# Quarter loads paced by PE steps in a sparse-attention and soft-MoE kernel on one Trainium2 core

## The chip, the cores and the metric

One core of a Trainium2 chip runs the kernel. The metric is device time in microseconds (us). Engine names follow the profile: PE is TensorE (PEld its weight load), DVE is VectorE, ACT is ScalarE, POOL is GpSimd, SP is SyncE, which issues every DMA here. "us from the start" counts from the first instruction of the profiled span.

## The reference, cut to what matters

The input is a block-sparse attention followed by a soft mixture of experts. All arrays are float32.

```python
# q, k, v: (4 batches, 8 heads, 768, 64); 24 blocks of 32 rows
mask = |block_i - block_j| <= 1, or block 0 or 23 on either side, or one of 3 sampled blocks
attn = softmax(where(mask, q @ k.T / 8, -1e9))
x = (attn @ v) as (3072 tokens, 512)
# soft MoE: 8 experts, 4 slots each; w1 (8, 512, 1024), w2 (8, 1024, 512)
logits = x @ phi                                  # (3072, 32)
slot_in = softmax(logits, over tokens).T @ x      # (32, 512)
slot_out[e] = relu(slot_in[e] @ w1[e]) @ w2[e]
out = softmax(logits, over slots) @ slot_out      # (3072, 512)
```

The weights w1 and w2 hold 33.5 MB; keys and values hold far less.

## The kernel before, in words

The program has two parts. In the first, 52 attention items (13 for each batch b: two "dense" halves, d0 and d1, for the first and the last block of queries, and 11 pairs of sparse query blocks) are computed while the tokens' logits and the slot sums run along. In the second, the expert weights go through PE and the result is combined and stored.

For a sparse pair, POOL and ACT copy the needed blocks of keys from `ktile` into a staging buffer `kst` (lines 365 to 380), PE multiplies (`s`, line 451), DVE takes the row maximum `nm` (466), ACT the exponential `p` (471), DVE turns it over into `ptt` (478), POOL copies sampled blocks of values into `vrs` (396), and PE forms `av` (529). DVE divides it into `x` (525), and PE turns `x` over (`mxt`, 692) for the logits (`ml`, 710) and the slot sums (`ms`, 760). For a dense item the names are `sd` (618), `pd` (637), `ptd` (641) and `avd` (529).

Everything that SP loads passes through its one queue in program order. SP's loads are tracked with eight semaphores in turn (DMAHW0 to DMAHW7 in the listings below), so a load waits until the eighth load before it has landed. These are the loads beside the attention:

- `q` (`load_q`, line 264): 128 KB for each of the 48 items, into four buffers. Each load waits for the PE step that last used the buffer.
- keys (`load_k`, line 274): four loads of 128 rows, 384 KB each, for a batch; two `ktile` buffers.
- values (`load_v`, lines 284 and 287): batches 0 and 1 in eight loads of 128 rows (455 KB, the last ones 260 KB); batches 2 and 3 in 16 loads of 32 rows (113.8 and 65 KB) from `vtab`. The buffers are `v_68` (batches 0 and 2) and `v_69` (1 and 3).
- weights (`load_w`, `load_wk`, line 179): pieces of 512 KB, 128 rows of 4 KB, 64 pieces in all. 22 of them are placed beside the attention: seven in `wpre`, and then, as buffers fall free in the last batch, three in a `ktile` buffer (`kw`), six in `v_68`, three in `ptd` and three in the other `ktile` buffer.

The order of the first part is made by a planner (`Plan.run`). Each task has an engine, an assumed cost, its dependencies, a key and buffers; the planner goes through assumed time and always takes the task that can start first. SP's tasks cost 0.45 to 0.47 us each there. The order that results is what each engine's queue holds, and it is fixed when the program is built.

Code behind the planner loads the other 42 pieces of weights. 15 of them have free room as the attention ends: nine in a pool `lwb`, which lies where the staging buffers of the attention were, and six in `v_69`. The other 27 wait for a buffer that the experts' matmuls (`pf`, line 1055, and `pso`, line 1063) have used up. SP's queue in this part is not written by hand: a scheduler sets the order.

Of the kernel before, what the change touches and what calls it, by code (L numbers as in the profile page):

```python
# [21 lines left out]
P = 128  # L22
NP = 4
# [12 lines left out]
NKST, NVR, NQ = 4, 6, 4  # L36
PB, PTB, XB, XTB = 4, 4, 6, 4
SB, MB = 4, 2

LD0, LD1 = 3, 12  # L40

CS = 2
CW = DM // CS
# [16 lines left out]
class Task:  # L60
    def __init__(self, f, opts, deps, key, acq, byte, pre):
        self.f, self.opts, self.deps, self.key = f, opts, [d for d in deps if d], key
        self.acq, self.byte, self.pre = list(acq), byte, pre
        self.start = self.fin = self.eng = None


class Plan:

    def __init__(self, pools, free):
        self.pools, self.free, self.tasks = pools, free, []

    def add(self, f, opts, deps, key, acq=(), byte=0, pre=None):
        t = Task(f, opts if isinstance(opts, list) else [opts], deps, key, acq, byte, pre)
        self.tasks.append(t)
        return t

    def run(self):
        tasks = self.tasks  # L80
        at = {e: 0.0 for e in LAG}
        dma = 0.0
        left = {t: len(t.deps) for t in tasks}
# [13 lines left out]
        while avail:  # L97
            best = None
            for t in avail:
                r, ok, k = ready[t], True, {}  # L100
                for p, _ in t.acq:
                    i = (nxt[p] + k.get(p, 0)) % self.pools[p]
                    k[p] = k.get(p, 0) + 1
                    if (p in queue and queue[p][0] is not t) or held[p][i]:
                        ok = False
                        break
                    r = max(r, slot[p][i])
                if ok:
                    for e, d in t.opts:
                        c = (max(r, at[e]), t.key, max(r, at[e]) + d)  # L110
                        if best is None or c < best[0]:
                            best = (c, t, e, d)
            assert best, [(t.key, t.opts) for t in avail][:8]
            (st, _, en), t, e, d = best
            avail.remove(t)
            t.start, t.eng, at[e] = st, e, en
            if e == "NONE":
                t.fin = st
            elif e == "SP":
                dma = max(dma, st + 1.4) + t.byte / 0.4e6  # L120
                t.fin = dma + 0.3
            else:
                t.fin = en
# [19 lines left out]

        todo = {e: [t for t in order if t.eng == e and t.pre] for e in at}
        for t in order:
            q = todo[t.eng]
            while q and q[0].start <= t.start + 1.6:
                u = q.pop(0)
                u.vals = u.pre(u.eng)
            t.f(t)  # L150


@with_exitstack
def attn_moe_kernel(ctx, tc, qT, kT, vfull, vtab, sampled, phi, w1, w2, out):
# [19 lines left out]

    def load_w(m, pool, t=None):
        if t is None:
            t = pool.tile([P, WP], F32, name=f"w{m}", tag="w")
        n, j = m // PW, m % PW
        SP.dma_start(out=t, in_=wsrc[n].rearrange("p c f -> p (c f)")[:, j * WP:(j + 1) * WP])
        wtile[m] = t.rearrange("p (c f) -> p c f", f=512 if n < 2 * NE else CW)  # L180

    wk = {}
# [8 lines left out]

    def load_wk(m, tag, j):

        load_w(m + j, None, wk[tag][:, j, :])

# [76 lines left out]

    def load_k(b, p):
        SP.dma_start(out=ktile[b][:, p, :], in_=kT[b, p])

# [3 lines left out]

    def load_v(b, cut, a):  # L280
        lo, hi = cut
        vb = vbuf[b % 2].rearrange("p (a f) -> p a f", a=2)
        if b < 2:
            SP.dma_start(out=vb[:, a, lo:hi], in_=vfull[b, :, a * VH + lo:a * VH + hi])
        else:
            s_ = slice(32 * a, 32 * a + 32)
            SP.dma_start(out=vb[s_, a % 2, lo:hi], in_=vtab[b - 2, s_, lo:hi])
        vtile[b] = vb.rearrange("p a (k r d) -> p a k r d", k=NBZ, r=2)

    def block_numbers(t, i, eng, most):  # L290
# [16 lines left out]
    plan = Plan(dict(s=SB, av=1, pt=MB, p=PB, ptt=PTB, kst=NKST, vrs=NVR, x=XB, xT=XTB, k=2, v=2, q=NQ,  # L307
                     ptd=1, lp=1, dT=1, d=1), free=("pt",))
# [26 lines left out]
    def plan_loads(b):  # L335

        a_k = add(lambda t: new_k(b), ("NONE", 0.0), [qks[first[b - 1] + LD0]] if b else [], -20, acq=[("k", k_use[b])])
        a_v = add(lambda t: None, ("NONE", 0.0), a_k.deps, -20, acq=[("v", v_use[b])])
        pieces = [("k", p) for p in range(NP)] + [("v", *c) for c in v_pieces(b)]
        ks, vs = [], []  # L340
        for m, c in enumerate(pieces):
# [4 lines left out]
            if c[0] == "k":  # L346
                ks.append(add(lambda t, c=c: load_k(b, *c[1:]), ("SP", 0.47), go + [a_k], key, byte=393216))
            else:
                vs.append(add(lambda t, c=c: load_v(b, *c[1:]), ("SP", 0.47), go + [a_v], key,
                              byte=455000 if b < 2 else 114000))  # L350
        t_k[b] = add(lambda t: None, ("NONE", 0.0), ks, -30)
# [899 lines left out]
```

## Time and profile before

| | |
|---|---|
| time, median of 3 runs | 346.43 us (344.92 to 349.33) |
| the profiled execution's own time | 341.82 us |
| its span, first to last instruction | 339.9 us |
| PE busy | 282.2 us, 83% |
| DVE, POOL, ACT busy | 216.7, 180.9, 164.2 us |
| mean granted PE clock | 0.942 |
| moved by DMA | 63.59 MB |
| attention part, to the last `av` | to 259.4 us from the start |
| experts, to the last weight piece's landing | to 320.4 us |

The page gives a share of the span for each engine; a stage has to be looked at by itself, since PE is almost full through the attention, and the DMA engines through the experts. In the chain of waits a piece named "issue" is time in which the engine had work in its program and no semaphore to wait for.

### The profile page before, as it was taken

The page shows a single profiled execution, that of the slowest core. Times are in us where ns is not written, and L with a number is a line of the kernel's source. Part 1 is how long each engine was busy: PE and PEld are TensorE (multiplying, and loading weights), DVE is VectorE, ACT ScalarE, POOL GpSimd, SP SyncE. Part 2 cuts the span into 40 slices and gives each one's busy share as a digit, 9 for nine tenths or more (in the row PEclk, how much of TensorE's full clock was granted, in tenths as well). Part 3 has the DMA queues.
Part 4 walks back from the last instruction along what each step waited for, and adds up shares of the span by engine and source line. Part 5 has one row for each costly group of instructions (what it writes and reads, how often), then busy time and mean ns, then how long its engine had stood idle before and what let it go on. Part 6 is the DMA issues. An engine that isn't in the chain of part 4 may idle for free.

```text
span 339.9 us, 17255 instructions
## 1 busy us (share of the span) xinstructions
PE 282.2 (83%) x7113; PEld 186.9 (55%) x7113; DVE 216.7 (64%) x495; ACT 164.2 (48%) x503; POOL 180.9 (53%) x505
## 2 busy tenths in 40 slices
PE   2697899995989989989999997699785859996650
PEld 0166676762767567776676665476563423453230
DVE  4696778769766998998887896639913430111250
ACT  2656567735646875466767373457500311013240
POOL 2686686984437997946999582648522132000000
PEclk9999999998979999999999999979987659999995
DMA  6942845300753240274341055970529948999987
GB/s 230 397 145 92 286 128 193 102 7 17 230 155 105 78 127 7 53 261 137 98 131 36 2 154 187 320 265 4 189 61 331 384 164 303 415 407 407 381 264 230
DMA packets 29152, 63.59 MB, mean 187 GB/s; under 512 B 3345, under 2 KB 15762, under 8 KB 29074
## 3 DMA queue, kind: packets, MB, share of 16 engines
q1 hardware_dynamic: 29074, 62.49, 54.3%
q8 instruction: 56, 0.92, 1.1%
q14 instruction: 22, 0.18, 0.2%
HBM read 56.19 MB, written 6.29 MB: 184 GB/s over the span
## 4 chain that ended last, share of the span: by engine, by line
PE 60%; DVE 15%; DMA 13%; issue 6%; ACT 2%; SPq 0%; ACTq 0%; POOL 0%; DVEq 0%
PE av L529 28%; PE s L451 11%; PE avd L529 7%; DMA w<-in_w_dram 5%; PE mxt L692 4%; DMA kw<-in_w_dram 3%; PE sd L618 3%; DMA v<-in_w_dram 3%; DVE ptt L478 2%; PE ml L710 2%; DVE ptd L641 2%; DVE nm L466 2%; DVE x L525 2%; DVE nm L630 2%; PE ms L760 1%
## 5 line engine op out<-in xcount | busy, mean ns | idle before, releaser
L396 POOL COPY vrs<-v 128x260 f32 x264 | 95.3, 408 | 31.2 <-PE av L529 24.7
L471 ACT ACTIVATE p<-s,nm 128x256 f32<-128x256 f32 x176 | 71.1, 478 | 16.7 <-DVE nm L466 15.8
L529 PE MATMUL av<-v,ptt 64*64 64x130 f32 (+2 forms) x1728 | 78.2, 294 | 0.4 <-issue 0.4
L478 DVE STREAM_TRANSPOSE ptt<-p 128x512 f32<-128x512 f32 x88 | 58.3, 692 | 17.7 <-ACT p L471 17.6
L529 PEld LDWEIGHTS av<-v,ptt 64*64 64x64 f32 (+2 forms) x1728 | 52.4, 136 | 27.5 <-issue 18.1
L451 PE MATMUL s<-kst,q 64*32 64x256 f32 x1408 | 55.1, 390 | 12.6 <-issue 7.1
L466 DVE TENSOR_REDUCE nm<-s 128x2 f32<-128x512 f32 x88 | 55.5, 677 | 4.7 <-PE s L451 4.3
L372 POOL COPY kst<-ktile 128x384 f32<-128x384 f32 x88 | 42.9, 510 | 20.2 <-PE s L451 17.5
L529 PE MATMUL av<-vrs,ptt 64*32 64x130 f32 x2112 | 45.2, 276 | 5.1 <-issue 5.1
L378 ACT ACTIVATE kst<-ktile 128x128 f32 x171 | 38.9, 302 | 20.3 <-PE s L451 11.0
L451 PEld LDWEIGHTS s<-kst,q 64*32 64x32 f32 x1408 | 30.4, 108 | 28.4 <-issue 13.1
L529 PEld LDWEIGHTS av<-vrs,ptt 64*32 64x32 f32 x2112 | 35.6, 106 | 6.0 <-issue 5.9
L303 ACT COPY xT<-mxt 128x512 f32<-128x512 f32 x20 | 11.7, 586 | 37.9 <-PE mxt L692 37.9
L529 PE MATMUL avd<-v,ptd 64*64 64x130 f32 x768 | 23.6, 271 | 5.0 <-issue 4.4
L637 ACT ACTIVATE pd<-sd,nb 128x384 f32<-128x384 f32 x32 | 16.8, 578 | 19.7 <-DVE nb L632 19.3
L529 PEld LDWEIGHTS avd<-v,ptd 64*64 64x64 f32 x768 | 21.8, 132 | 7.3 <-issue 2.7
L380 POOL COPY kst<-ktile 128x128 f32 x93 | 23.6, 297 | 1.5 <-ACT kst L378 0.7
L618 PE MATMUL sd<-ktile,q 64*32 64x384 f32 x256 | 18.0, 523 | 7.4 <-DMA ktile<-in_kT_dram 6.0
L692 PE MATMUL mxt<-ident,x 128*128 128x128 f32 x96 | 16.8, 301 | 4.0 <-DVE x L525 2.7
L523 DVE TENSOR_SCALAR rs<-av 128x8 f32<-128x8 f32 (+1 forms) x28 | 4.5, 160 | 23.5 <-PE av L529 23.4
L630 DVE TENSOR_REDUCE nm<-sd 128x1 f32<-128x384 f32 x32 | 16.2, 544 | 4.8 <-PE sd L618 4.7
L415 POOL TENSOR_SCALAR q<-q 128x256 f32<-128x256 f32 x21 | 8.5, 407 | 19.4 <-DMA q<-in_qT_dram 19.4
(117 smaller groups left out, 271.2 us busy)
## 6 DMA issues: line engine op xcount, KB each, us to landing
w<-in_w_dram SPq DMA_DIRECT2D x28, 512.0 KB, 7.9
v<-in_w_dram SPq DMA_DIRECT2D x18, 512.0 KB, 6.5
q<-in_qT_dram SPq DMA_DIRECT2D x48, 128.0 KB, 2.7
ktile<-in_kT_dram SPq DMA_DIRECT2D x16, 384.0 KB, 4.7
kw<-in_w_dram SPq DMA_DIRECT2D x12, 512.0 KB, 8.0
v<-in_vfull_dram SPq DMA_DIRECT2D x12, 455.0 KB, 6.1
out_dram<-ob SPq DMA_DIRECT2D x20, 256.0 KB, 4.2
ptd<-in_w_dram SPq DMA_DIRECT2D x6, 512.0 KB, 9.5
```

Source lines behind the costliest of these rows:

```text
L372: POOL.tensor_copy(out=st[:, :, w:w + 96], in_=kv[:, :, (i - 1) * BLK:(i + 2) * BLK])
L378: ACT.activation(out=st[:, :, o:o + BLK], in_=src, func=AF.Copy, scale=1.0)
L380: POOL.tensor_copy(out=st[:, :, o:o + BLK], in_=src)
L396: POOL.tensor_copy(out=st[:, :, j:j + 1, :], in_=vf[:, :, ds(t.vals[j], 1), :])
L451: PE.matmul(u.s[r][32 * p:32 * p + 32, j, :], lhsT=u.q[s_, p, j, :], rhs=kd[j][0][s_, p, :], start=True, stop=True)
L466: DVE.tensor_reduce(out=u.nm[r], in_=u.s[r], axis=AX.X, op=ALU.max, negate=True)
L471: ACT.activation(out=u.p[r][:, j, :], in_=u.s[r][:, j, :], func=AF.Exp, bias=u.nm[r][:, j:j + 1], scale=1.0)
L478: DVE.transpose(out=T.pt[r][:, :, 2 * w:2 * w + 2, :].rearrange("p k j q -> p j k q"), in_=u.p[r].rearrange("p j (k q) -> p j k q", k=8))
L529: PE.matmul(av[o:o + m, g, r * 2 * D1:(r + 1) * 2 * D1].rearrange("p (a d) -> p a d", a=2), lhsT=lhsT, rhs=rhs, start=start, stop=stop)
L618: PE.matmul(u.s[r][k][32 * p:32 * p + 32, :], lhsT=T.dq.q[s_, p, j, :], rhs=kt[s_, p, 384 * k:384 * (k + 1)], start=True, stop=True)
L630: DVE.tensor_reduce(out=nm[:, k:k + 1], in_=u.s[r][k], axis=AX.X, op=ALU.max, negate=True)
L692: PE.transpose(T.px[:, c, :], T.x[:, c * P:(c + 1) * P], ident)
```

## The change

Three things change, and the planner's order with them.

1. The keys of batches 1 to 3, the values of batch 1 and the 22 weight pieces beside the attention are cut into four loads of 32 rows each (`LR = 32`): 96 KB for keys, about 114 or 65 KB for values, 128 KB for weights. Batch 0 stays as it was, and the values of batches 2 and 3 had 32 rows already. SP issues 336 loads where it issued 210.
2. In the planner, a task marked `pace` may not start before the last paced one's start plus its bytes at 0.22 MB per us (`RATE`).
3. A paced load gets a dependency on the last PE step that ends, in the planner's time, by the load's start. The later one of the two `ktile` groups of weights is cut up, though not paced.

```diff
+LR, RATE = 32, 0.22
...
                 if ok:
+                    if t.pace:
+                        r = max(r, paced)
...
             t.start, t.eng, at[e] = st, e, en
+            if t.pace:
+                paced = st + t.byte / RATE / 1e6
...
+        pe = []
         for t in order:
...
-            t.f(t)
+            i = t.f(t)
+            if t.eng == "PE":
+                last = next(i for i in reversed(self.tc.nc.cur_bb.bb.instructions) if i.engine == E_.PE)
+                pe.append((t.fin, last.name))
+            elif t.pace:
+                name = [n for f, n in pe if f <= t.start][-1]
+                self.tc.add_manual_dep(i.ins, name, mybir.DependencyInfo(
+                    mybir.DependencyClass.Sync, mybir.DependencyReason.DATA), reason="pace")
...
-    def load_k(b, p):
-        SP.dma_start(out=ktile[b][:, p, :], in_=kT[b, p])
+    def load_k(b, p, rows):
+        return SP.dma_start(out=ktile[b][rows, p, :], in_=kT[b, p, rows])
...
+        rs = [slice(r, r + LR) for r in range(0, P, LR)] if b else [slice(0, P)]
+        pieces = [("k", p, r) for p in range(NP) for r in rs]
+        pieces += [("v", *c, r) for c in v_pieces(b) for r in (rs if b < 2 else [None])]
...
     for m in range(NPRE):
-        add(lambda t, m=m: load_w(m, wpre), ("SP", 0.45), [qks[max(4, (N - 4) * (m + 1) // (NPRE + 1))]], N + m, byte=524288)
+        for r in range(0, P, LR):
+            add(lambda t, m=m, r=r: load_w(m, wpre, None, slice(r, r + LR)), ("SP", 0.45),
+                [qks[max(4, (N - 4) * (m + 1) // (NPRE + 1))]], N + m + r / P, byte=4096 * LR, pace=True)
...
         for j in range(KW[tag]):
-            add(lambda t, m=m, tag=tag, j=j: load_wk(m, tag, j), ("SP", 0.47), go(j) + [a_w], N + m + j, byte=524288)
+            for r in range(0, P, LR):
+                add(lambda t, m=m, tag=tag, j=j, r=r: load_wk(m, tag, j, slice(r, r + LR)), ("SP", 0.47), go(j) + [a_w],
+                    N + m + j + r / P, byte=4096 * LR, pace=tag != "ktile" or n0 < 12)
```

Three places show what this does to the queues. In the listings a row is one instruction, with its line (line numbers differ by 18 to 27 between the two files), what it writes and reads, and the semaphores that it waits for.

The first is SP's queue where the keys of batch 2 are loaded. Before:

```order
L264 DMA q<-in_qT_dram 128x256 [waits DMAHW6_49,PE_49,Activation_49]
L274 DMA ktile<-in_kT_dram 128x768 [waits DMAHW7_49]
L274 DMA ktile<-in_kT_dram 128x768 [waits DMAHW0_49]
L264 DMA q<-in_qT_dram 128x256 [waits DMAHW1_49,PE_49,Pool_49]
L274 DMA ktile<-in_kT_dram 128x768 [waits DMAHW2_49]
L274 DMA ktile<-in_kT_dram 128x768 [waits DMAHW3_49]
L287 DMA v_68<-in_vtab_dram 32x910 [waits DMAHW4_49,Pool_49]
```

And now:

```order
L283 DMA q<-in_qT_dram 128x256 [waits DMAHW0_49,PE_49,Pool_49]
L293 DMA ktile<-in_kT_dram 32x768 [waits DMAHW1_49,Activation_49]
L293 DMA ktile<-in_kT_dram 32x768 [waits DMAHW2_49,PE_49]
L283 DMA q<-in_qT_dram 128x256 [waits DMAHW3_49,Pool_49]
L293 DMA ktile<-in_kT_dram 32x768 [waits DMAHW4_49]
L293 DMA ktile<-in_kT_dram 32x768 [waits DMAHW5_49]
L293 DMA ktile<-in_kT_dram 32x768 [waits DMAHW6_49]
L293 DMA ktile<-in_kT_dram 32x768 [waits DMAHW7_49]
L293 DMA ktile<-in_kT_dram 32x768 [waits DMAHW0_49]
L293 DMA ktile<-in_kT_dram 32x768 [waits DMAHW1_49]
L283 DMA q<-in_qT_dram 128x256 [waits DMAHW2_49,PE_49,Activation_49]
```

The four loads became 16, of which eight stand ahead of the last `q` shown and the others behind it. A second paced load carries the wait for PE that the `q` load behind it had; most of the others need no PE wait of their own, since an earlier wait in the same queue covers it.

The second is the end of SP's loads beside the attention. Before (`kw` and `v_69` hold weights here, `w_6992` is the first piece of `lwb`):

```order
L179 DMA kw<-in_w_dram 128x1024 [waits DMAHW7_49]
L179 DMA v_69<-in_w_dram 128x1024 [waits DMAHW0_49,Pool_49]
L179 DMA v_69<-in_w_dram 128x1024 [waits DMAHW1_49]
L179 DMA v_69<-in_w_dram 128x1024 [waits DMAHW2_49,PE_49]
L179 DMA v_69<-in_w_dram 128x1024 [waits DMAHW3_49,PE_49]
L179 DMA v_69<-in_w_dram 128x1024 [waits DMAHW4_49,PE_49]
L179 DMA w_6992<-in_w_dram 128x1024 [waits DMAHW5_49,PE_49]
```

And now (`w_7118` is the first piece of `lwb`, `w_7134` the ninth):

```order
L197 DMA kw<-in_w_dram 32x1024 [waits DMAHW5_49]
L197 DMA w_7118<-in_w_dram 128x1024 [waits DMAHW6_49,PE_49,Pool_49]
L197 DMA w_7120<-in_w_dram 128x1024 [waits DMAHW7_49]
L197 DMA w_7122<-in_w_dram 128x1024 [waits DMAHW0_49]
...
L197 DMA w_7134<-in_w_dram 128x1024 [waits DMAHW6_49]
L197 DMA v_69<-in_w_dram 128x1024 [waits DMAHW7_49]
L197 DMA v_69<-in_w_dram 128x1024 [waits DMAHW0_49]
```

Five of the six `v_69` pieces stood ahead of the nine `lwb` pieces; now all six stand behind them. The PE step that the first `lwb` piece waits for is, in both programs, among the last five matmuls of the last `av`.

The third is PE's queue where it first reads the keys of batch 1. Before:

```order
L618 MATMUL sd<-ktile,q 32x384 [waits DMAHW5_49]
L618 MATMUL sd<-ktile,q 32x384
L618 MATMUL sd<-ktile,q 32x384 [waits DMAHW6_49]
L618 MATMUL sd<-ktile,q 32x384
L618 MATMUL sd<-ktile,q 32x384 [waits DMAHW0_49]
```

And now:

```order
L641 MATMUL sd<-ktile,q 32x384 [waits DMAHW6_49,DMAHW5_49]
L641 MATMUL sd<-ktile,q 32x384 [waits DMAHW1_49,DMAHW0_49]
L641 MATMUL sd<-ktile,q 32x384 [waits DMAHW3_49,DMAHW2_49]
L641 MATMUL sd<-ktile,q 32x384 [waits DMAHW5_49,DMAHW4_49]
L641 MATMUL sd<-ktile,q 32x384 [waits DMAHW7_49,DMAHW6_49]
```

Each matmul of a new key tile waits for two quarters where one of two waited for one load. In the whole program PE gets 64 more such wait instructions, 29 of them in the attention and 34 ahead of the experts' first matmuls. Otherwise PE's order of work differs at a few places by one step (an `mxt`, `md` or `sd` moved past its neighbour), and those of DVE, ACT and POOL likewise.

More of the change, by code (lines that the diff above doesn't have):

```diff
@@ L60, with __init__ @@
 class Task:
-    def __init__(self, f, opts, deps, key, acq, byte, pre):
+    def __init__(self, f, opts, deps, key, acq, byte, pre, pace):
+        self.pace = pace
         self.f, self.opts, self.deps, self.key = f, opts, [d for d in deps if d], key
@@ L67, with __init__, add @@
 class Plan:
[L71 to L75, printed above, removed]
+    def __init__(self, tc, pools, free):
+        self.tc, self.pools, self.free, self.tasks = tc, pools, free, []
+    def add(self, f, opts, deps, key, acq=(), byte=0, pre=None, pace=False):
+        t = Task(f, opts if isinstance(opts, list) else [opts], deps, key, acq, byte, pre, pace)
         self.tasks.append(t)
@@ L81, in run @@
         at = {e: 0.0 for e in LAG}
-        dma = 0.0
+        dma = paced = 0.0
         left = {t: len(t.deps) for t in tasks}
@@ L173, in attn_moe_kernel, with load_w @@
     wtile = [None] * NW
-    def load_w(m, pool, t=None):
-        if t is None:
+    def load_w(m, pool, t=None, rows=slice(0, P)):
+        if wtile[m] is None and t is None:
             t = pool.tile([P, WP], F32, name=f"w{m}", tag="w")
+        elif t is None:
+            t = wtile[m].rearrange("p c f -> p (c f)")
         n, j = m // PW, m % PW
-        SP.dma_start(out=t, in_=wsrc[n].rearrange("p c f -> p (c f)")[:, j * WP:(j + 1) * WP])
+        i = SP.dma_start(out=t[rows], in_=wsrc[n].rearrange("p c f -> p (c f)")[rows, j * WP:(j + 1) * WP])
         wtile[m] = t.rearrange("p (c f) -> p c f", f=512 if n < 2 * NE else CW)
+        return i
     wk = {}
@@ L190, in new_wk, with load_wk @@
             wk[tag] = buf[:, 0:k * WP].rearrange("p (k f) -> p k f", k=k)
-    def load_wk(m, tag, j):
-        load_w(m + j, None, wk[tag][:, j, :])
+    def load_wk(m, tag, j, rows=slice(0, P)):
+        return load_w(m + j, None, wk[tag][:, j, :], rows)
     def w_of(n, c):
@@ L278, in v_pieces, with load_v @@
         return [(c, a) for c in cuts for a in range(2 if b < 2 else NP)]
-    def load_v(b, cut, a):
+    def load_v(b, cut, a, rows):
         lo, hi = cut
@@ L283, in load_v @@
         if b < 2:
-            SP.dma_start(out=vb[:, a, lo:hi], in_=vfull[b, :, a * VH + lo:a * VH + hi])
+            i = SP.dma_start(out=vb[rows, a, lo:hi], in_=vfull[b, rows, a * VH + lo:a * VH + hi])
         else:
             s_ = slice(32 * a, 32 * a + 32)
-            SP.dma_start(out=vb[s_, a % 2, lo:hi], in_=vtab[b - 2, s_, lo:hi])
+            i = SP.dma_start(out=vb[s_, a % 2, lo:hi], in_=vtab[b - 2, s_, lo:hi])
         vtile[b] = vb.rearrange("p a (k r d) -> p a k r d", k=NBZ, r=2)
+        return i
     def block_numbers(t, i, eng, most):
@@ L305, in evac @@
             DVE.tensor_copy(out=out, in_=in_)
-    plan = Plan(dict(s=SB, av=1, pt=MB, p=PB, ptt=PTB, kst=NKST, vrs=NVR, x=XB, xT=XTB, k=2, v=2, q=NQ,
+    plan = Plan(tc, dict(s=SB, av=1, pt=MB, p=PB, ptt=PTB, kst=NKST, vrs=NVR, x=XB, xT=XTB, k=2, v=2, q=NQ,
                      ptd=1, lp=1, dT=1, d=1), free=("pt",))
@@ L346, in plan_loads @@
             if c[0] == "k":
-                ks.append(add(lambda t, c=c: load_k(b, *c[1:]), ("SP", 0.47), go + [a_k], key, byte=393216))
+                ks.append(add(lambda t, c=c: load_k(b, *c[1:]), ("SP", 0.47), go + [a_k], key, byte=393216 // len(rs),
+                              pace=b > 0))
             else:
                 vs.append(add(lambda t, c=c: load_v(b, *c[1:]), ("SP", 0.47), go + [a_v], key,
-                              byte=455000 if b < 2 else 114000))
+                              byte=455000 // len(rs) if b < 2 else 114000, pace=b > 0))
         t_k[b] = add(lambda t: None, ("NONE", 0.0), ks, -30)
```

1 line of the change is left out of this document (removed).

## The prediction

> **What bounds the kernel now.** I began with the page. PE is nearly full through the attention, and the last quarter belongs to DMA. The question is what stops PE. The chain of waits tells it: apart from DVE stretches it runs through PE, with pieces called "issue", in which PE had nothing to wait for (start us, us, what; beside them some `av` pieces for comparison).
>
> ```profile
> 26.52 2.10 issue
> ...
> 40.22 1.18 issue
> ...
> 43.04 4.73 PE av L529 x174
> ...
> 54.42 0.37 issue
> ...
> 93.05 1.74 issue
> ...
> 96.31 5.96 PE av L529 x174
> ...
> 105.18 2.35 PE av L529 x88
> ...
> 126.23 0.33 issue
> ...
> 150.48 0.99 issue
> ...
> 203.21 2.33 issue
> ...
> 217.72 3.15 issue
> ...
> 222.94 3.43 PE av L529 x88
> ...
> 243.28 2.33 issue
> ...
> 245.61 4.38 PE av L529 x92
> ...
> 256.49 2.42 issue
> ```
>
> The ten pieces sum to 16.94 us, all on the chain that sets the end. What was SP doing then? Its timeline has large loads just ahead of them:
>
> ```profile
> 199.16 0.42 SPq L179 DMA_DIRECT2D w<-in_w_dram  x1
> ...
> 200.58 1.33 SPq L179 DMA_DIRECT2D kw<-in_w_dram  x2
> ...
> 222.02 0.33 SPq L264 DMA_DIRECT2D q<-in_qT_dram  x1
> ...
> 237.89 1.28 SPq L179 DMA_DIRECT2D kw<-in_w_dram  x3
> 251.68 4.55 SPq L179 DMA_DIRECT2D v<-in_w_dram  x5
> ```
>
> PE has to fetch its program too. By the page's queues and its busy row, that is queue q8:
>
> ```profile
> PE 282.2 (83%) x7113; PEld 186.9 (55%) x7113; DVE 216.7 (64%) x495; ACT 164.2 (48%) x503; POOL 180.9 (53%) x505
> ...
> q8 instruction: 56, 0.92, 1.1%
> ```
>
> 14226 PE and PEld instructions by 56 fetches are 254 to a fetch, 16 KB each. The DMA view of 198.8 to 203.2 us, ahead of a stop, has data and no row for q8:
>
> ```profile
> q1 hardware_dynamic: 338, 0.87, 68.7%
> issues: line engine op xcount, KB each, median us to landing
> ```
>
> The same view of 203.2 to 205.6, the stop itself, has the fetch, and PE goes on as that stretch ends:
>
> ```profile
> q1 hardware_dynamic: 299, 0.74, 89.2%
> q8 instruction: 1, 0.02, 2.4%
> ```
>
> Now the opposite case, 161 to 175 us, with eight loads of 32 rows, four of `q` and one weight piece:
>
> ```profile
> q8 instruction: 4, 0.07, 2.0%
> ...
> q<-in_qT_dram SPq DMA_DIRECT2D x4, 128.0 KB, 2.4
> w<-in_w_dram SPq DMA_DIRECT2D x1, 512.0 KB, 3.9
> v<-in_vtab_dram SPq DMA_DIRECT2D x4, 113.8 KB, 2.7
> ```
>
> Four fetches came and the chain has no stop there. So I read the stops as code fetches that came late behind several large loads in flight at once.
>
> [...]
>
> **The change, part by part.** The profiled execution took 341.82 us, 1.9 more than its span; the sum is made against that. The median of the runs is 346.43, 4.61 higher, and I add this at the end.
>
> *The stops.* In SP's new order at most ten paced loads stand between two `q` loads, and SP needs some 0.42 us to issue one, as for the `w` load above. What does a piece of 512 KB take when the engines are full? Two views of the experts' part, SP's timeline and the chain:
>
> ```profile
> 259.35 6.42 SPq L179 DMA_DIRECT2D w<-in_w_dram  x9
> ...
> 278.99 4.18 SPq L179 DMA_DIRECT2D w<-in_w_dram  x5
> ...
> 297.17 2.83 SPq L179 DMA_DIRECT2D kw<-in_w_dram  x3
> ```
>
> ```profile
> 281.27 6.88 DMA w<-in_w_dram
> ...
> 310.20 10.18 DMA w<-in_w_dram
> ```
>
> SP goes at the pace of landings there: the issues step by 1.25 to 1.28 us ((2.83 - 0.33) / 2 for `kw`). From the third of the 27 pieces, landed at 288.15, to the last at 320.38 the mean is 1.34. A quarter of a piece is 0.32 to 0.34 us of work, issued every 0.42, so no queue builds up; three whole pieces issued in 1.28 us are 3.8 to 4.0 us of work and do build one. The last stop, at 256.49, stood behind `v` pieces that are now queued behind the last `av`. The pace itself changes less: most quarters go out where the whole load went. Bounds: all 16.94 us gone, or none. I take a rest of 0.35 us for each of the ten, as at 54.42 and 126.23: gain 13.4.
>
> *The slow clock.* Three stops are followed by a stretch at half the clock, such as this one from 221.9 to 225.3 (after the busy times: PEclk, DMA share, GB/s); the rows below it serve the next item.
>
> ```profile
> 221.90:225.30 3.40, 3.40 (x38) 2.50 (x44) 1.91 (x3) 2.32 (x9) 3.00 (x9) 0.50 1.00 320
> ```
>
> ```profile
> 72.00:86.00 14.00, 10.47 (x275) 6.05 (x261) 12.37 (x31) 5.87 (x13) 8.69 (x24) 0.88 0.05 14
> 110.00:123.00 13.00, 12.32 (x386) 8.01 (x366) 11.95 (x26) 10.76 (x39) 11.17 (x32) 1.00 0.38 109
> 123.00:163.00 40.00, 38.51 (x1176) 27.52 (x1174) 35.66 (x84) 24.40 (x74) 29.62 (x85) 1.00 0.36 108
> ```
>
> `av` x174 took 5.96 there against 4.73, x88 3.43 against 2.35, and x92 4.38 against 2.46 (2.35 by 92/88): 4.2 us. The stops at 26.52 and 203.21 had no such sequel, so it isn't sure that a stop alone decides. Bounds 0 and 4.2; I take two thirds, 2.8.
>
> *Given back to DVE.* In the three stretches just shown DVE is busy 12.37 of 14, 11.95 of 13 and 35.66 of 40 us. What PE gains before 163 us is 6.71 of stops less 2.1 of rest, and 0.8 of clock: 5.4. PE may then wait for DVE instead. Bounds 0 and 5.4; a third: loss 1.8.
>
> *New waits on PE.* 64 more, of 51 ns by the row for `av`:
>
> ```profile
> L529 PEldq EVENT_SEMAPHORE  x27: 51/51/1096, 17.5 to 240.6; - x27
> ```
>
> The 34 ahead of the experts hide under the weights' arrival (uncovered: 1.7 us). The 29 in the attention have no cover, since PE is full: loss 1.5.
>
> *`q` behind paced loads.* Twelve or so `q` loads now stand one issue behind a quarter that waits for the same PE step: 0.42 us each, 5 in all. POOL and ACT wait for `q`, then `kst` or `p`, then PE. They are busy 53% and 48%, and `q` itself lands behind shorter loads, so most is covered, and a gain of as much can't be excluded. Bounds -5 to 5; loss 1.0.
>
> *126 more issues on SP.* At 0.42 us these are 53 us of SP, which waits most of the time. After the last `q` load, which went out at 222.02, 38 quarters stand ahead of the `lwb` pieces: 16 us, done well before the last `av` at 259. Cost none; if SP took 0.8 us each, the experts' weights would be late by what passes 259.
>
> *The order at the end.* Before, five `v` pieces went out from 251.68 and nine of `w` from 259.35, and then the engines ran dry: the next issue, at 278.99, waited for the experts' first matmuls. Now all 42 pieces begin at the last `av`. Fifteen of them keep the engines busy until 3.9 + 14 x 1.34 = 22.7 us past the start (3.9 is the landing of the one weight piece in the quiet window), while the experts' first matmuls free buffers 19.6 us past it. So the stream should not run dry, and the last piece lands 3.9 + 41 x 1.34 = 58.8 us after the first issue, against 320.4 - 259.35 = 61.0. Bounds: 0, if the stream breaks at that seam; 4.6, if every step takes 1.28. Gain 2.2.
>
> Sum: -13.4 - 2.8 + 1.8 + 1.5 + 1.0 - 2.2 = -14.1, so 327.7 in the profiled execution's terms and **332.3 us** as a median.
>
> **The rivals.**
>
> *DVE becomes the bound.* All 5.4 us before 163 are given back, 3.6 more than in the sum: 335.9. For it speak the three DVE rows; against it, that the larger stops lie after 198, where DVE has room.
>
> *The stops stay.* If it isn't the queue of large loads but the mere share of busy DMA engines that delays a fetch, the same bytes delay it as before. Then gains of stops, clock and the DVE term fall away: 346.4 - 2.2 + 1.5 + 1.0 = 346.7. The window 161 to 175 speaks against it, though its DMA load is light.
>
> [...]
>
> [...]
>
> [...]
>
> **How the numbers follow.** Chances: the forecast 0.58, DVE as bound 0.18, the stops stay 0.13, slower 0.11. The predicted time is the forecast's. All gains at their best are 16.94 + 4.2 + 4.6 = 25.8, or 320.6; I take 320.5 as the lower end. The upper end, 347, takes in the rival in which the stops stay, and leaves out the slower one. The forecast's own range is 323 to 340. Two per cent, about what can be told from no change, is 339.5 and 353.4. Faster: nearly all of the forecast and most of the DVE case, 0.73. Within: the stops' case and some of the others, 0.17. Slower: 0.10.
>
> **What would show it.** Right: "issue" pieces before 260 us sum to under 5 us; PEclk shows no half-clock stretch near 96, 222 and 246; the last `av` ends 10 to 14 us sooner; the weight stream has no break between the 15th piece and the 16th. Wrong: "issue" pieces of over 1 us beside bursts of quarters (the stops stay); DVE stretches of the chain longer by what PE gained (DVE); 32-row loads landing in 5 us or more, with POOL or ACT waiting longer for `q` than before (slower); or the last `av` sooner and the end not.

## The result, and the profile after

Four runs of the changed kernel took 327.54 to 331.0 us, median **328.5 us**; the kernel before, run beside them, had a median of 347.27 us. The ratio on record is **0.967, 95% interval 0.960 to 0.9745**. The medians themselves would give 0.946, and against the medians of before in the three batches of experiments (341.88, 345.14 and 343.24 us) 328.5 is 0.952 to 0.961. The profiled executions went from 341.82 to 327.54 us, 14.3 us less, where the prediction's sum had 14.1; the median fell by 18.8 because the runs of before lie up to 7.5 us above its profiled one, those of the change at most 3.5 above. Disturbed runs are left out of all ratios, which leaves two runs of four for the cut without the pace (332.41 and 328.18), and the profiled execution of the change without `q` loads (323.84) is such a run.

Is it PE's stops that went? The waits of PE up to 262 us, summed by what ended them (us in total, times, longest us), first of before, then of the change:

```profile
PE s L451 <- issue: 7.1, 4, 3.1
...
PE av L529 <- issue: 5.4, 4, 2.4
PE avd L529 <- issue: 4.4, 2, 2.3
```

```profile
PE av L552 <- issue: 1.0, 3, 0.5
...
PE s L474 <- issue: 0.7, 2, 0.6
...
PE avd L552 <- issue: 0.2, 1, 0.2
```

16.9 us became 1.9. The same stretch of work that held the stop of 2.33 us now runs with a burst of quarters beside it. SP's timeline of the change there, and the DMA view of 196 to 206 us:

```profile
196.15 2.16 SPq L197 DMA_DIRECT2D w<-in_w_dram  x2
...
199.77 5.95 SPq L197 DMA_DIRECT2D kw<-in_w_dram  x10
```

```profile
q1 hardware_dynamic: 835, 1.79, 64.1%
q8 instruction: 2, 0.03, 1.7%
...
kw<-in_w_dram SPq DMA_DIRECT2D x10, 128.0 KB, 4.0
```

Ten quarters take 0.6 us of SP each, and two code fetches (q8) come through in the view's 10 us; in before none came in the 4.4 us ahead of the stop.

The granted clock: windows of the change at places where the same view of before had 0.88, 0.93, 0.94 and 0.94 (the last three numbers of a row are PEclk, DMA share, GB/s):

```profile
72.00:86.00 14.00, 10.98 (x336) 7.49 (x340) 11.97 (x30) 5.92 (x13) 10.06 (x29) 1.00 0.10 30
86.00:110.00 24.00, 23.17 (x714) 17.06 (x710) 18.18 (x38) 16.29 (x56) 14.92 (x43) 1.00 0.53 154
...
198.00:225.00 27.00, 25.20 (x742) 17.93 (x734) 19.53 (x41) 16.48 (x58) 15.92 (x46) 1.00 0.80 211
225.00:246.00 21.00, 18.95 (x608) 13.72 (x600) 14.46 (x36) 9.81 (x31) 9.06 (x25) 1.00 0.60 164
```

All are 1.00. The engines were no less busy: between 198 and 225 us before had a DMA share of 0.78, the change has 0.80. By the trace's own records the last `av` ends at 246.04 us instead of 259.35 (13.3 sooner) and the last weight piece lands at 305.89 instead of 320.38 (14.5 sooner).

What took PE's place on the chain of waits? The page's shares of the span (the rows of before had PE 60%, DVE 15%, DMA 13%, issue 6%), and four pieces of the chain itself:

```profile
PE 43%; DMA 23%; DVE 14%; issue 5%; ACT 4%; POOL 3%; POOLq 2%; SPq 1%; ACTq 1%; DVEq 0%
```

```profile
41.74 3.68 DMA q<-in_qT_dram
...
95.25 2.16 issue
...
108.03 3.78 DMA q<-in_qT_dram
...
205.82 4.24 DMA q<-in_qT_dram
```

Loads of `q` now stand on the chain; before had none ahead of 250 us. The "issue" piece at 95.25 is POOL's (a `kst` copy ahead of it, a `vrs` copy behind it), not a stop of PE. DVE's share of the chain went from 15% to 14%. The chain is not the same as what PE itself waited for; the point on what was given back, below, comes to that.

### The profile page after: what moved, and what is told of

The parts are those of the page before. It is cut to its first block, busy times and chain, and to the rows that moved or that the text cites. A ratio compares the mean times of both kernels' runs of the same rounds, so it can differ in the third digit from the quotient of the medians.

```text
span 325.7 us, 17510 instructions
## 1 busy us (share of the span) xinstructions
PE 278.9 (86%) x7113; PEld 184.9 (57%) x7113; DVE 216.0 (66%) x496; ACT 162.7 (50%) x502; POOL 180.0 (55%) x505
## 4 chain that ended last, share of the span: by engine, by line
PE 43%; DMA 23%; DVE 14%; issue 5%; ACT 4%; POOL 3%; POOLq 2%; SPq 1%; ACTq 1%; DVEq 0%
PE av L552 19%; PE s L474 8%; DMA w<-in_w_dram 6%; PE avd L552 5%; PE sd L641 4%; DMA q<-in_qT_dram 4%; DMA kw<-in_w_dram 3%; DVE ptt L501 3%; DMA v<-in_w_dram 3%; DMA ptd<-in_w_dram 3%; PE mxt L715 3%; ACT p L494 2%; DVE nm L489 2%; DVE x L548 2%; POOLq L311 2%
## 5 line engine op out<-in xcount | busy, mean ns | idle before, releaser
L552 PE MATMUL av<-v,ptt 64*64 64x130 f32 (+2 forms) x1728 | 74.9, 285 | 1.4 <-DVE x L548 1.3
L552 PEld LDWEIGHTS av<-v,ptt 64*64 64x64 f32 (+2 forms) x1728 | 50.2, 131 | 27.1 <-issue 19.7
L474 PE MATMUL s<-kst,q 64*32 64x256 f32 x1408 | 53.3, 380 | 6.4 <-POOL kst L395 2.3
L474 PEld LDWEIGHTS s<-kst,q 64*32 64x32 f32 x1408 | 29.4, 106 | 21.6 <-issue 4.6
L641 PE MATMUL sd<-ktile,q 64*32 64x384 f32 x256 | 19.9, 511 | 7.4 <-DMA ktile<-in_kT_dram 5.9
L436 ACT ACTIVATE q<-q 128x256 f32<-128x256 f32 x27 | 11.3, 420 | 19.8 <-DMA q<-in_qT_dram 16.5
L715 PE MATMUL mxt<-ident,x 128*128 128x128 f32 x96 | 16.1, 287 | 5.8 <-DVE x L548 3.8
L715 PEld LDWEIGHTS mxt<-ident,x 128*128 128x128 f32 x96 | 10.1, 140 | 16.2 <-DVE x L548 7.4
## 6 DMA issues: line engine op xcount, KB each, us to landing
v<-in_w_dram SPq DMA_DIRECT2D x12, 512.0 KB, 10.9
```

The costliest lines, as they stand in the source:

```text
L474: PE.matmul(u.s[r][32 * p:32 * p + 32, j, :], lhsT=u.q[s_, p, j, :], rhs=kd[j][0][s_, p, :], start=True, stop=True)
L552: PE.matmul(av[o:o + m, g, r * 2 * D1:(r + 1) * 2 * D1].rearrange("p (a d) -> p a d", a=2), lhsT=lhsT, rhs=rhs, start=start, stop=stop)
L641: PE.matmul(u.s[r][k][32 * p:32 * p + 32, :], lhsT=T.dq.q[s_, p, j, :], rhs=kt[s_, p, 384 * k:384 * (k + 1)], start=True, stop=True)
L715: PE.transpose(T.px[:, c, :], T.x[:, c * P:(c + 1) * P], ident)
```

## The experiments

The theory: PE's code fetches stand behind the bytes that are queued ahead of them; a fetch that comes later than the block in hand lasts stops PE (a block is what one fetch brings, 254 of PE's instructions by before's 14226 in 56 fetches); quarters keep the queue short. The rivals of the prediction, and others formed on the way, stand in the expectations. Except where said, what is compared is the sum of PE's waits for "issue" up to 262 us, and the time's ratio to before in the same batch. In four runs (whole loads with pace, columns, halves without and with pace) that sum holds 1.35 us near 75 us which is a wait for DVE: PE goes on 0.10 us after an `x` of DVE ends, as in the runs in which the same wait is put down to DVE. Without it their sums, in this order, are 12.7, 1.7, 10.0 and 10.9.

**The cut without the pace.**

```diff
-        self.pace = pace
+        self.pace = False
```

> The loads are cut in quarters as in the change, but no rate is kept in the plan and no load waits for a PE step. Theory (code fetches come late when several large loads are queued at once): SP's own issues, about 0.55 us each in the change's trace, hold a burst of 128 KB quarters below what the engines can carry, so no depth builds up; 'issue' pieces of PE before 262 us sum to 1 to 4 us (1.45 with the pace, 16.94 before), time 326 to 331. Rival (it is the share of busy DMA engines that delays a fetch, and the pace that lowers it): the stops come back by half or more, 8 to 17 us, time 337 to 347.

Measured: 328.18 and 332.41 us (all four runs have a median of 333.24) against a median of 341.88 for before, too few for an interval. The waits for "issue" sum to 4.0 us (1.9 in the change, 16.9 in before). The cut alone removes three quarters of the stops. The rival, that it is the share of busy engines which delays a fetch and the pace that lowers it, falls: between 198 and 225 us the share was 0.85 here, higher than in before (0.78). SP's own issues were not the only brake in this run: from 212 to 231 us the trace has 16 issues that began only as the eighth load ahead had landed, up to 0.39 us late. In the change no issue between 20 and 250 us did.

**The pace without the cut.**

```diff
-LR, RATE = 32, 0.22
+LR, RATE = 128, 0.22
```

> The loads stay whole (512 and 384 KB), but the plan keeps the rate of 0.22 MB/us and each load waits for a PE step, so that two of them are 1.8 to 2.4 us apart. Theory: a whole load is about 1.3 us of work for the engines, so that at that distance no two are queued together; a fetch stands behind 1.3 us at most, which its lead of a block mostly covers: 'issue' pieces sum to 2 to 6 us, time 328 to 334. Rival (the size of the single load matters, not their number at once): stops of 1 us and more stay at half of the old places, sum 8 us or more, time 337 to 345.

Measured: 335.29 us, ratio 0.981 (0.972 to 0.990). The stops stayed, 14.0 us: a miss for the theory's number. The chain shows them, and SP's timeline shows why:

```profile
203.63 2.19 issue
218.51 1.47 issue
...
252.52 1.76 issue
```

```profile
199.47 0.42 SPq L197 DMA_DIRECT2D w<-in_w_dram  x1
...
200.42 8.65 SPq L197 DMA_DIRECT2D kw<-in_w_dram  x3
...
211.25 5.75 SPq L197 DMA_DIRECT2D v<-in_w_dram  x3
```

Ahead of 203.63 `w` and two of the three `kw` still went out together (199.47, 200.42 and 200.90 by the trace): the steps that they waited for were already over when SP came to them. Ahead of 218.51 the three `v` went out at 211.25, 213.60 and 216.68, spaced as the plan wanted, and landed 4.6 to 5.2 us later, each still on its way when the next was issued. So a rate in the plan does not by itself space the loads on the chip, and whole loads that are spaced so still queue up.

**Quarters by columns.** Each load has 128 rows and a quarter of their length (weights shown; keys and the values of batch 1 likewise).

```diff
-        i = SP.dma_start(out=t[rows], in_=...[rows, j * WP:(j + 1) * WP])
+        i = SP.dma_start(out=t[:, cols(rows, 0, WP)], in_=...[:, cols(rows, j * WP, (j + 1) * WP)])
```

> Quarters of the same bytes and pace, but cut by columns: 128 rows each and a quarter of the row's length. Theory (bytes queued at once): as the change, 'issue' pieces 1 to 4 us, 326 to 332, the upper end if the four times shorter rows make the engines slower. [...] Rival of the other sign (32 rows are slow by themselves and cost something in the change): 128 rows land over 0.5 us sooner than the quarters of 32 rows, and the time is 2 us or more below the change's 328.5.

Measured: 328.95 us, ratio 0.963 (0.9575 to 0.968), waits of 3.1 us. `ktile` quarters landed in 3.2 us (median) against 3.1 with 32 rows, `kw` quarters in 3.8 in both. The rival does not hold: 32 rows are no worse than 128 rows of a quarter of the length, and no better. Whether shorter rows cost something that 32 rows cost too, this run can't tell.

**The last group whole.** The three last weight pieces of the attention go uncut.

```diff
-            for r in range(0, P, LR):
+            lr = LR if n0 < 12 else P
+            for r in range(0, P, lr):
```

> The change, but the last three weight pieces of the attention (second group in the keys' buffer) are left whole, 512 KB each, three issued within 1.3 us. Theory: one stop of 2.0 to 2.5 us returns within 8 us of their issue near 235 us, its fetch comes some 200 instructions later than its neighbours, and a half-clock stretch may follow it (up to 2 us); the rest stays as in the change; profiled execution 2 to 4.5 us longer than the change's 327.5, and none of the stops before 200 us returns. Rival (three loads at once are nothing special, the gain came from elsewhere): no stop over 0.6 us there, time within 0.8 us of the change's.

Measured: 330.09 us, ratio 0.964 (0.957 to 0.970), and no stop of the forecast size. A miss, for which windows between two code fetches show a reason. First this kernel from one fetch to the next, behind it the same stretch of before (us, then PE's busy time with its count, PEld's):

```profile
231.36:237.26 5.90, 5.08 (x143) 3.62 (x140) 4.50 (x12) 2.33 (x7) 2.74 (x8) 1.00 0.96 244
```

```profile
235.91:243.16 7.25, 7.25 (x242) 5.56 (x238) 7.08 (x17) 4.54 (x13) 5.96 (x17) 1.00 0.56 207
```

A fetch brings 254 instructions (14226 by 56). Before, PE ran 480 in the 7.25 us between two fetches and then stood still; here it ran 283 in 5.90 us, because it also waited for DVE and POOL. The fetch came late here too, but PE had not used up what it had. This run could not decide between theory and rival at that place; the next one was put where PE is full.

**The first group whole.** Four pieces near 200 us go uncut and unpaced, the rest is the change.

```diff
-        for r in range(0, P, LR):
+        lr = LR if m < NPRE - 1 else P
+        for r in range(0, P, lr):
...
-            for r in range(0, P, LR):
+            lr = P if n0 == 3 else LR
+            for r in range(0, P, lr):
```

> The change, but four weight pieces near 200 us (the last one ahead of the attention's end buffers and the first group in the keys' buffer) are whole and without pace, as before, issued within about 2 us. Theory: one stop of 1.8 to 2.5 us returns within 6 us of them, its fetch some 200 instructions later than its neighbours; as after the stop at 203.21 of before no half-clock stretch is needed; no other stop over 1.1 us returns; last av 1.5 to 2.5 us later than the change's 246.0, time 329.5 to 332. Rival (the stop belongs to PE's work at that place, not to the loads): no stop over 0.6 us within 198 to 210 us.

Measured: 333.18 us, ratio 0.969 (0.959 to 0.980). By this ratio the time can't be told from the change's 0.967; what decides is the profiled execution. SP's timeline, the chain, and the windows around the stop:

```profile
199.46 0.43 SPq L197 DMA_DIRECT2D w<-in_w_dram  x1
199.98 1.46 SPq L197 DMA_DIRECT2D kw<-in_w_dram  x1
...
201.97 0.90 SPq L197 DMA_DIRECT2D kw<-in_w_dram  x2
```

```profile
205.71 0.98 PE s L474 x20
206.69 3.19 issue
209.88 1.18 PE s L474 x14
```

```profile
206.70:209.41 2.71, 0.00 (x0) 0.00 (x0) 0.65 (x3) 0.47 (x3) 0.22 (x1) 0.99 0.74 268
209.41:212.83 3.42, 2.95 (x45) 1.93 (x46) 1.37 (x3) 0.71 (x3) 1.65 (x4) 0.51 0.20 70
```

The stop is back, 4.3 us behind the last of the four, 3.19 us long and followed by 3.4 us at half the clock, and there is no other of PE over 0.6 us. The DMA view of 202 to 206.7 us, ahead of the stop, has data and no fetch of PE's (q8), as before:

```profile
q1 hardware_dynamic: 409, 1.15, 83.9%
q14 instruction: 1, 0.01, 0.5%
```

The last `av` ends at 251.87, 5.8 later than the change's: more than forecast, since the stop is longer and the clock went with it (3.19 and half of 3.4 make 4.9). This is the run that ties the stops to the loads: whole pieces at one place bring one stop back at that place, and no other. Does the fetch wait behind data, or is it asked for late? Its request is in no trace, but its start can be set against the number of instructions that PE has run (256 to a fetch, counting the semaphore waits too: 14361 in before by 56 fetches). In before, 13 fetches between 30 and 250 us had next to no data in the 3 us ahead of them (a DMA share under 0.05); they started 0 to 103 instructions behind the earliest such count. The fetches of the four longest stops, and the one here, started 256 instructions behind it, which is 3.6 to 5.4 us and all that PE had left to run. So the start moves with the data ahead of it. That speaks for waiting, though it does not prove it.

**Halves without the pace.**

```diff
-LR, RATE = 32, 0.22
+LR, RATE = 64, 0.22
...
-        self.pace = pace
+        self.pace = False
```

> Halves of 64 rows (256 and 192 KB) instead of quarters, no rate in the plan and no waits for PE steps. Theory (a fetch goes through behind the bytes already queued, and the quarters help because SP, at about 0.55 us an issue, cannot put out 128 KB pieces as fast as the engines move them): halves come out at 256 KB by 0.55 us, faster than they are moved (three whole pieces landed 1.28 us apart, 0.64 us a half), so depth builds up again in the bursts: 'issue' pieces of PE before 262 us sum to 7 to 14 us, time 333 to 341. Rival (only the size of the single load counts, a fetch comes between two loads): a half is 0.6 us of wait, inside the lead of a block, sum below 5 us, time 328 to 334.

Measured: 344.69 us, ratio 1.001 (0.9955 to 1.007), waits of 11.3 us; the sum as the theory had it, the time worse than either said. SP's timeline, and the chain's largest pieces:

```profile
206.24 3.66 SPq L197 DMA_DIRECT2D kw<-in_w_dram  x6
```

```profile
211.56 1.83 issue
217.99 3.07 issue
226.17 3.40 issue
```

Six halves go out in 3.66 us, 256 KB each 0.61 us, which is 430 GB/s. The DMA view of 206 to 211.5 us has data on the engines for 94.3% of the time, and they moved 223 GB/s:

```profile
DMA packets 474, 1.23 MB, mean 223 GB/s; under 512 B 83, under 2 KB 211, under 8 KB 472
...
q1 hardware_dynamic: 472, 1.20, 94.3%
```

So SP hands out about twice what is moved in that stretch, and the queue grows. Quarters come out at 220 GB/s (128 KB each 0.6 us), and the change's window 198 to 225 moved 211 at a share of 0.80. That the wait of a single half is short did not help, so the rival falls. Both stops over 3 us were again followed by 3.4 us at half the clock. A single wait of PE for DVE of 4.9 us at 127.6, with 6.8 us at half the clock from 130.4 on, which the change does not have, is part of the lost time; its cause is open.

**Halves with the pace.**

```diff
-LR, RATE = 32, 0.22
+LR, RATE = 64, 0.22
```

> Halves of 64 rows with the rate of 0.22 MB/us and the waits. Theory: a half each 1.2 us where the waits bite leaves no depth, but in the whole-load run the waits held back only some of the bursts (three pieces still went out within 1.5 us at 199 and at 234 us), so 'issue' pieces sum to 3 to 8 us, less than in the halves without pace; time 329 to 335. Rival (the pace does nothing, cutting everything): the sum and the time are those of the halves without pace, within 1 us and 2 us.

Measured: 339.88 us, ratio 0.987 (0.977 to 0.996). The waits, 12.2 us, are no less than without the pace, and so miss the theory's 3 to 8, as the time misses its 329 to 335; but they are many and short (the longest 1.73 us against 3.40). The pace splits long stops into short ones, which leaves the clock alone: the profile has no half-clock stretch in the attention, that of the halves without pace has three.

**The old order at the end.** Five of the six pieces for the values' second buffer go ahead of the nine for the new pool.

```diff
+    m0, tag = len(wpool) + NLB, LATEW[1]
+    new_wk(tag)
+    for j in range(5):
+        load_wk(m0, tag, j)
     next_w([lwb] * NLB)
-    load_group(LATEW[1])
+    load_wk(m0, tag, 5)
+    wpool.extend([Group(tag)] * KW[tag])
```

(`load_wk` adds the piece's number within the group.)

> The change, but at the end five of the six pieces in the values' second buffer stand ahead of the nine of the new pool again, as before. Theory: these five whole pieces go out before the last av, from some 8 us ahead of it, and bring back one stop of 2 to 2.5 us there (256.49 in before); behind the last av the stream is as before: the last piece lands 61 us after it instead of 59.8, since the engines run dry until the experts' first matmuls; time 2 to 5 us over the change's 328.5. Rival (the order is worth nothing, or the earlier start of five pieces, 6.4 us of transfer, carries through to the end): no stop over 0.6 us there or an end that is earlier, time 324 to 328.5.

Measured: 330.57 us, ratio 0.959 (0.946 to 0.972). No stop of the forecast size came back (the longest is 0.7 us), and the last piece landed 58.2 us after the last `av`, sooner than in the change (59.8) where 61 was forecast. SP's timeline:

```profile
247.11 2.48 SPq L197 DMA_DIRECT2D v<-in_w_dram  x5
249.69 10.17 SPq L197 DMA_DIRECT2D w<-in_w_dram  x9
```

The buffer came free only 1.9 us ahead of the last `av` (248.97), too late to disturb a fetch; before it was 7.7 us. And the stream did not run dry. The median lies in the theory's range (330.5 to 333.5), but the ratio is below the change's and the stop is missing. So the rival was right here: the order is worth nothing that can be seen.

**The change, and the kernel before, without `q` loads.** In both, all `q` loads but the first four are left out, and later pairs work on the old buffers, scaled once more.

```diff
+        n = nq[0]
+        nq[0] += 1
+        if n < NQ:
+            qb.append(pst.tile([P, NP, 2, BLK], F32, name=f"q{n}"))
+            SP.dma_start(out=qb[n], in_=qT[b, g])
+        return qb[n % NQ]
```

> The change with the loads of q left out but for the first four (later pairs work on the old buffers, scaled again; the output is not the reference's). Theory: what the removed stops gave before 185 us was taken back by q, which lands 3 to 4 us after its issue between quarters (two pieces of 3.7 us on the change's chain of waits, none in before); without q the time is 6 to 10 us below the change's, 0.94 to 0.95 of before, and the third batch's sd block starts 4 to 7 us sooner than the change's 181.4. Rival (DVE took it back, as the prediction had it): DVE pieces take q's place on the chain, time within 3 us of the change's, 0.958 to 0.968 of before.

> The kernel before with the same loads of q left out (its output is not the reference's). Theory: in before q is covered by PE's stops and full PE, its chain has no q piece ahead of 250 us, so that q is worth only 0 to 4 us there (0.988 to 1.0 of before), clearly less than in the change; the stops remain, 10 to 17 us of 'issue' pieces. Rival (q costs the two kernels the same): the gain is within 2 us of that of the change without q.

Measured: the change without `q` loads 319.42 us, ratio 0.933 (0.928 to 0.9385); the kernel before without `q` 338.55 us, ratio 0.9875 (0.975 to 1.000). So `q` is worth 9 to 12 us in the change (328.5 - 319.4 = 9.1 by the medians of two batches, (0.967 - 0.933) x 343 = 11.7 by their ratios) and 4.3 in before (0.0125 x 343; 0 to 8.6 by its interval). The stops of before stay without `q`, 15.3 us. The chain's shares on the page of the change without `q` loads:

```profile
PE 62%; DVE 16%; DMA 14%; issue 2%; ACT 2%; SPq 0%; ACTq 0%; POOL 0%; DVEq 0%
```

PE is the chain again; POOL and `q` are gone from it, and DVE, which the rival had in their place, has 16% where the change had 14. The `sd` block of batch 3, the last, started at 178.4 instead of 181.4: 3.0 us sooner in that execution, not 4 to 7. Since 5.8 MB of transfers left with these loads, and 44 issues of SP, the 9 to 12 us are an upper bound for the lateness of `q` alone.

**`q` on ACT's queue.**

```diff
-        SP.dma_start(out=q, in_=qT[b, g])
+        ACT.dma_start(out=q, in_=qT[b, g])
```

and `q` is planned on ACT.

> The change with q issued by ACT instead of SP, so that no q load stands behind a waiting quarter in SP's order and it has a queue of its own. If a q load then passes the quarters in flight it lands in 2 to 2.5 us, the waits of POOL and ACT for q fall from 29 us to under 18, and the time is 322 to 327, below the change. Rivals: it lands as late as before because it shares the engines (time 327 to 331); or the issue and the wait for a free q buffer stand in front of ACT's own work and cost more than q's lateness did (time over 332).

Measured: 335.59 us, ratio 0.981 (0.971 to 0.992). The page's row of these loads (the change's has 2.9):

```profile
q<-in_qT_dram ACTq DMA_DIRECT2D x48, 128.0 KB, 3.3
```

A queue of its own brings `q` in later, not sooner. The waits of POOL and ACT for it between 14 and 246 us sum to 25.2 us (29.8 in the change), not to under 18. ACT now has "issue" waits of its own, 9.4 us in sum up to 262 us (2.7 in the change), the longest 2.9, and PE's waits for ACT's `pd` went from 1.7 to 6.6 us. PE's own "issue" waits rose as well, from 1.9 to 6.3, which neither rival had and no run explains. So both rivals have a part, and they are not all.

**A slower pace.**

```diff
-LR, RATE = 32, 0.22
+LR, RATE = 32, 0.16
```

> The change with the plan's rate at 0.16 MB/us instead of 0.22: a 128 KB quarter each 0.8 us where the waits bite, instead of 0.55 to 0.6, which SP reaches anyway. Theory: fewer quarters in flight when a q load or a fetch comes, q's waits fall by 3 to 8 us in sum, 'issue' pieces stay under 3 us, time 325 to 329 (0.955 to 0.967 of before). Rival: the weights come too late, the last quarters stand beside the last av and push the new pool's pieces back by 2 to 6 us: 330 to 335.

Measured: **326.02 us, ratio 0.951 (0.940 to 0.962)**, the lowest of all versions that do the whole work, though the interval overlaps the change's. The window that stood at 0.80 is lighter, and PE busier in it:

```profile
198.00:225.00 27.00, 25.92 (x774) 19.09 (x774) 20.84 (x44) 18.15 (x63) 17.68 (x50) 1.00 0.62 173
```

"Issue" waits are 2.0 us. The waits for `q` between 14 and 246 us hardly fell (29.1 us against 29.8), which misses that part of the expectation, but the longest became shorter, 2.2 us against 3.5 in the change:

```profile
ACT q L436 <- DMA q<-in_qT_dram: 14.7, 13, 2.2
POOL q L438 <- DMA q<-in_qT_dram: 12.2, 10, 1.8
```

The weights were not late: the last `av` ends at 242.7.

## Why the prediction was right, point by point

*The stops*, -13.4 in the sum: 16.9 became 1.9, so -15.0. The reason held. The first group whole brought one stop back by four loads alone, the cut without pace kept the stops away, and the halves, which leave SP twice as fast (430 GB/s in a burst against 220), brought them back. The queue itself can be read from the traces: take the bytes that SP has issued and subtract those that the DMA engines have begun. From 24 us after the start until 8 us ahead of the last `av` this never passed 0.38 MB in the change, 0.40 with the slower pace, 0.49 by columns and 0.53 in the cut without the pace, and these runs have 1.7 to 4.0 us of stops. It reached 1.01 MB in the halves with pace, 1.43 without, 1.63 with whole paced loads and 2.17 in before, and these have 10.0 to 16.9. In the first group whole it was 1.70 at 202.9 us, 3.8 us ahead of its one long stop; in the last group whole 1.52 at 235.4, where PE was not full.

What failed is a detail of the working: a whole piece was taken as 1.3 us of work, from landings at the end of the kernel. In the attention, single whole pieces landed 4.6 to 5.2 us after their issue and overlapped at 2.4 to 3.1 us distance; on that the expectation of the pace without the cut went wrong. For the quarters two errors cancel. At 211 GB/s for a share of 0.80 a quarter is 0.50 us of work beside the attention (an estimate), not 0.32 to 0.34, and more than the 0.42 that the prediction has for its issue. The queue stays short because SP needs 0.6 us in a burst.

*The slow clock*, -2.8: the three stretches near 96, 222 and 246 us are gone, 4.2 us of them by the prediction's own working; the bound was nearer than the value. A fourth stretch of before, 82.0 to 85.4 us, is not in the sum, though it makes the 0.88 in the prediction's row of 72 to 86. It came with a wait of 3.48 us for ACT, not with a stop for code, and is gone with it (1.67 in the change). All stops and waits of PE of over 3 us past the start, in before, in the first group whole and in the halves without pace, were followed by 3.4 us or more at half the clock. Of the stops near 2.3 us in before one was (243.28) and one not (203.21), while one of 1.74 us was (93.05), and in the cut without the pace a stretch at 219.8 had no stop over 1.1 us ahead of it. Each of the four stretches of before up to its last `av` lasts 3.41 us by the trace's clock records, behind stops and waits of 1.74 to 3.48 us. What parted the two equal stops, no run here shows.

*Given back*: 15.0 and 4.2 make 19.2 us, and the last `av` moved by 13.3, so 5.9 were given back where DVE, PE's waits and `q` had 1.8 + 1.5 + 1.0 = 4.3. PE's own account up to the last `av` splits it; PE's busy time, and the largest of its waits for DVE, first of before, then of the change:

```profile
0.00:259.36 259.36, 226.06 (x6574) 158.60 (x6574) 195.63 (x430) 148.07 (x466) 172.87 (x489) 0.97 0.45 144
...
PE mxt L692 <- DVE x L525: 2.7, 4, 1.3
```

```profile
0.00:246.05 246.05, 224.57 (x6574) 157.53 (x6574) 195.14 (x431) 146.61 (x465) 172.01 (x489) 1.00 0.50 143
...
PE mxt L715 <- DVE x L548: 3.8, 7, 1.5
PE av L552 <- DVE x L548: 1.3, 1, 1.3
```

The busy time fell by 1.5 us only, so that 2.7 of the 4.2 us do not show up there; why, no run tells. PE's waits for others rose by 3.4 us, from 15.6 to 19.1. Those that DVE ended rose by 3.2, from 3.0 to 6.2, so the term on DVE (1.8) was too small rather than wrong. What it had wrong is the reason. It saw DVE as full, but DVE's share of the chain did not rise: at 108.03 and 205.82 the chain goes back past DVE's steps to `q`, sized at 1.0 with bounds of -5 to 5. The working asked whether `q` lands later (2.9 us for 2.7: hardly) and whether POOL and ACT wait longer for it (29.8 us for 29.6 between 14 and 246: no). It did not ask what had covered those waits. PE's stops had, as the two runs without `q` bear out: `q` is worth 4.3 us in before and at most 9 to 12 in the change, though the one interval reaches 8.6. It is not all of it, since 4.3 us of waits for DVE are left in the change without `q`.

By place, -4.0 us came by the `sd` block of batch 3 (185.4 to 181.4) and -9.3 from there to the last `av`, as the larger stops lie there. The three stops within batch 0, 3.7 us, brought 1.8 by the start of batch 1's `avd` (85.8 to 84.0); the rest stays open.

*New waits on PE*, 1.5: no run isolates them. They come from the cut and not from the pace: up to the last `av` the trace has 148 of PE's semaphore waits in the change and in the cut without the pace alike, 120 in before.

*SP's issues*, 0: the last quarter went out at 240.67, ahead of the last `av`. *The end*, -2.2: 61.0 became 59.8, so -1.2. The order can't be seen to have done it: the old order gave 58.2, and other runs with the change's end gave 58.6 (columns) to 61.3 (slower pace).

*What would show it*: the clock, the last `av` (13.3 us, forecast 10 to 14) and the unbroken weight stream came as written. The criterion of "issue" pieces under 5 us holds for PE (1.9); on the chain itself the pieces of 0.3 us and more sum to 6.3, of which PE has 0.9 and POOL 5.1 (2.16 and 1.76 among them). With the many shorter pieces it is 15.1, the page's 5%, for 19.3 in before. The criterion should have named the engine and the least length.

*The rivals*: stops that stay were excluded by the cut without pace; loads of 32 rows that are slow by themselves (the chance of 0.11) by the columns, where `ktile` quarters landed in 3.2 us against 3.1 with 32 rows. No run shows a cause that would make 32 rows slow. DVE as the bound came in with 3.2 us of PE's waits instead of 5.4, and with `q` ahead of it on the chain.

*The median*: profiled execution 327.54 against 327.7 forecast; the 4.61 us added for the median were 0.96 in the change (328.5 - 327.54), which is nearly all of the difference between 332.3 and 328.5. That the sum itself is off by only 0.2 us is luck: its terms missed by -1.6 (stops), -1.4 (clock), +1.6 (given back) and +1.0 (the end), which cancel to -0.4.

## What to carry to other kernels

A full engine with short stops that nothing explains may be waiting for its own code: count its instructions between two fetches on the instruction queue (here 370 to 486 ahead of the eight longest stops, where a fetch brings 254), and look for bursts of large loads ahead of the longest of them. What helped here was to hand out loads no faster than the engines moved them: quarters at 220 GB/s in a burst left 1.9 us of stops with the pace, halves at 430 without it 10.0, and before had 16.9. Cutting them so that the issuing engine itself is the brake was enough here (4.0 us without the pace), and a planned rate for whole loads was not (12.7). When a stop of the full engine goes, ask which other engine's waits had been hidden by it, since these are next.

## What the runs showed of the hardware

SP does not need the same time for each issue. Most quarters take 0.42 us, but by the trace about every seventh issue between 196 and 238 us takes 1.2 to 1.8, as this one in the change:

```profile
206.24 1.36 SPq L197 DMA_DIRECT2D kw<-in_w_dram  x1
```

So a long burst costs 0.6 us an issue (5.95 for ten, above), not the 0.42 of the prediction. A fetch may be late without a stop: in the change the most that PE ran between two fetches was 360 instructions, in before 370 to 486 ahead of its eight longest stops, where a fetch brings 254 (counted over the records of PE and PEld). At all ten stops of before PE went on 2.2 to 2.6 us after the fetch had started, so a stop is long because the start is late. And the DMA engines, 94.3% busy, moved 223 GB/s beside the attention in the halves (206 to 211.5 us), and 320 at a share of 1.00 in before (221.9 to 225.3), though the page of the change has 407 to 412 for the experts' part:

```profile
GB/s 219 403 134 142 182 211 181 153 22 17 124 141 178 137 123 29 20 133 186 173 118 119 2 20 150 238 213 200 199 156 194 382 412 407 407 408 409 380 255 233
```

Why busy engines move less beside the attention was not tried.
